# Logit products of the first layer issued four hidden units at a time, and Gelu written over its own input in a ring of nine tiles

## The chip, the core and the metric

The program runs on one NeuronCore of a Trainium2 chip. Five engines each work through their own instruction list: PE (TensorE, matrix products, with PEld for its weight loads), DVE (VectorE), ACT (ScalarE), POOL (GpSimd) and SP (SyncE, which issues DMAs). They meet only at semaphores. The metric is the device time of one execution in microseconds (us): 1949.1 us before the change, the median of three runs (1948.05 to 1950.38).

## The reference, cut to what matters

```
X  = real(fft(fft(x, axis=1), axis=2))       # x: 8 x 3072 x 256
h  = X.reshape(8*3072, 256) @ w_in           # 256 -> 2048, the first layer
g  = h * sigmoid(1.702 * h)                  # Gelu, sigmoid form
y  = g @ w_out                               # 2048 -> 256
logits = y @ w_gate                          # 8 experts
# each token goes to its best expert (capacity 768 per expert, the first tokens win),
# which computes relu(y @ w1[e]) @ w2[e], scaled by the softmax weight
```

Only tokens that an expert keeps need the second layer in full. So the program first computes just the logits of all 24,576 tokens (with `wog = w_out @ w_gate`, 2048 x 8), routes, and then recomputes the kept tokens.

## The kernel before, in words

The start (to about 93 us) loads the tables and transforms the first batch. Phase 3 (from about 1098 us) gathers the kept tokens and runs both layers for them. Between them lies phase 2, where the change is: for 8 batches of four blocks it computes the hidden values and the logits, while the transform of the next batch and the routing of the last one are threaded in between by a timetable (`pre` and `post`, numbered by unit). There is no scheduler: every engine runs its instructions in the order in which the Python code issues them.

A block holds 384 columns (385 in the fourth). One *unit* (`m1_unit`) is one of 16 slices of 128 hidden features over the block's columns. On PE it is three matmuls into a bank `pe` (L744; a fourth, L746, where a table of modes says 2) and three into a bank `po` (L749). There are two banks of each. Then `e` is formed by ACT (L752, mode 2) or DVE (L754, mode 1), and DVE writes `h = e + po` and `h = e - po` (L756, L757), 2 x 384 values. One unit later ACT issues Gelu (L763, `m1_gelu`), from a ring of three tiles `h` into a ring of six tiles `g`.

The logit products (`m1_logits`, L772) are four matmuls for a pair of units: 8 logits, padded to 32 weight columns, so each uses a strip of 32 of the array's 128 columns, and the four (two units, two signs) go to the four strips and accumulate in one bank `acc` over the block's eight pairs. The operands are float32, and the trace shows each such matmul as two instructions, so eight per pair. `flush_logits` issues one pair; the loop calls it after every odd unit, 256 times in all, for the pair whose Gelu was issued by then. After a block's last pair ACT copies `acc` out (`m1_evac`, L782).

Other names that the timetable puts between units on PE: L523 (`pf`, the transform), L707 and L709 (`psuv`, transposes of the next block's input), L722 (`psb`), L810 (`psL`) and L844 (`psp`), both routing, L425 and L431 (`pss`, a scale).

Of the kernel before, what the change touches and what calls it, by code (L numbers as in the profile page):

```python
# [10 lines left out]
F32 = mybir.dt.float32  # L11
# [11 lines left out]
P = 128  # L23
# [37 lines left out]
SEQ0 = (("uee", "vee", "row", "ueo", "veo", "w", "uo", "w"), ("vo",))  # L61
TICKS, WAIT0 = range(0, 13, 2), (2, 0, 1, 0, 1, 0, 1, 0)
AGE = (0, 2, 4, 5)


def split16(t):
# [113 lines left out]
class K:  # L180
# [128 lines left out]
    def first_folds(self):  # L309

        nc = self.nc
        ve, ge = nc.vector, nc.gpsimd
        o = FOFF
        xs = [self.xt.pop((0, i)) for i in range(6)]
        r = self.xr.pop(0)
        for i, x in enumerate(xs + [r]):
            n = P if i < 6 else 12
            jk = self.hp.tile([P, 2, 386], F32, tag="h", bufs=3, name="jk").rearrange("p s n -> p (s n)").bitcast(F16)
            v = x.rearrange("p s d -> p (s d)") if i < 6 else x
            nc.scalar.activation(jk[:n, :v.shape[1]], v, AF.Abs, accum_out=self.acc[:n, i:i + 1])  # L320
            yield
        scale = self.fft_scale(0)
        late = []
        for c in range(3):
            pe, mo, m, a = [self.xp.tile([P, 2, 2, w], F32, tag=nm, bufs=n, name=nm)
                            for nm, w, n in (("pe", UW, 1), ("mo", VW, 2), ("m", XW, 2), ("a", XW, 1))]
            eu, ev = [self.xp.tile([P, 2, w], F32, tag=nm, bufs=n, name=nm) for nm, w, n in (("eu", UW, 2), ("ev", VW, 1))]
            f = self.f[0, c] = self.fp.tile([P, FW], F32, tag="f", bufs=3, name="f")
            two = lambda k: f[:, o[k]:o[k + 1]].rearrange("p (s n) -> p s n", s=2)

            def op(e, out, x, y, sub):
                e.tensor_tensor(out, x, y, op=ALU.subtract if sub else ALU.add)
                if c == 2 and e is ve:
                    next(scale, None)

            for z in range(2):
                x = xs[2 * c + z]
                op(ge if z else ve, m[:, z], x[:, :2], x[:, 2:], True)
                op(ve, a[:, z], x[:, :2], x[:, 2:], False)
            for fn in late:  # L340
                fn()
            late = []
            op(ve, pe, a[:, :, :, :UW], a[:, :, :, UW:], False)
            if c == 2:
                op(ve, mo, m[:, :, :, 1:1 + VW], m[:, :, :, UW + 1:UW + 1 + VW], True)
            op(ve, eu, pe[:, :, 0], pe[:, :, 1], False)
            e = ge if c == 2 else ve
            op(e, two(0), pe[:, :, 0], pe[:, :, 1], True)
            e = ge if c == 1 else ve
            op(e, f[:, o[2]:o[3]], eu[:, 0], eu[:, 1], False)  # L350
            op(e, f[:, o[3]:o[4]], eu[:, 0], eu[:, 1], True)
            if c < 2:
                op(ve, mo, m[:, :, :, 1:1 + VW], m[:, :, :, UW + 1:UW + 1 + VW], True)

            def odd(c=c, f=f, mo=mo, ev=ev, two=two(1)):
                e = ve if c == 2 else ge
                op(ge, two, mo[:, :, 0], mo[:, :, 1], False)
                op(e, ev, mo[:, :, 0], mo[:, :, 1], True)
                op(e, f[:, o[4]:o[5]], ev[:, 0], ev[:, 1], True)
                op(e, f[:, o[5]:o[6]], ev[:, 0], ev[:, 1], False)  # L360

            if c == 1:
                late.append(odd)
            else:
                odd()
            del f
        for _ in scale:
            pass
        fr = self.f[0, 3] = self.fp.tile([12, UW + VW], F32, tag="fr", name="fr")
        ge.tensor_tensor(fr[:, :UW], r[:, :UW], r[:, UW:], op=ALU.add)  # L370
        ge.tensor_tensor(fr[:, UW:], r[:, 1:1 + VW], r[:, UW + 1:UW + 1 + VW], op=ALU.subtract)
        yield
        for _ in self.fft_split(0):
            pass
# [359 lines left out]
    def m1_unit(self, b, i, f):  # L734


        nc = self.nc
        n, n2 = self.blk(i)
        x = self.uvt[b, i]
        mode = (MODES0 if b == 0 else MODES7 if b == B - 1 else MODES)[NFC * i + f]  # L740
        fs = slice(f * P, (f + 1) * P)
        pe = self.peo.tile([P, 512], F32, tag="pe", bufs=EB, name="pe")
        for q, (a, c) in enumerate(((0, 0), (0, 1), (1, 0))):
            nc.tensor.matmul(pe[:, :n2], self.G[:, 0, a, fs], x[:, 0, c, :n2], start=(q == 0), stop=(q == 2 and mode != 2))  # L744
        if mode == 2:
            nc.tensor.matmul(pe[:, :n2], self.g3[:, fs], self.u3[b, i][:, :n2], start=False, stop=True)  # L746
        po = self.peo.tile([P, 512], F32, tag="po", bufs=EO - EB, name="po")
        for q, (a, c) in enumerate(((0, 0), (0, 1), (1, 0))):
            nc.tensor.matmul(po[:, :n2], self.G[:, 1, a, fs], x[:, 1, c, :n2], start=(q == 0), stop=(q == 2))  # L749
        e = self.ocp.tile([P, 386], F32, tag="e", bufs=3, name="e")  # L750
        if mode == 2:
            nc.scalar.activation(e[:, :n], pe[:, :n], AF.Copy)  # L752
        else:
            nc.vector.scalar_tensor_tensor(e[:, :n], self.ub[b, i][:, :n], self.cf[:, f:f + 1], pe[:, :n], op0=ALU.mult, op1=ALU.add)  # L754
        h = self.hp.tile([P, 2, 386], F32, tag="h", bufs=3, name="h")
        nc.vector.tensor_tensor(h[:, 0, :n], e[:, :n], po[:, :n], op=ALU.add)  # L756
        nc.vector.tensor_tensor(h[:, 1, :n], e[:, :n], po[:, :n], op=ALU.subtract)  # L757
        return h

    def m1_gelu(self, b, i, f, h):  # L760
        n, n2 = self.blk(i)
        g = self.gp.tile([P, 2, 386], F32, tag="g", bufs=6, name="g")
        self.nc.scalar.activation(g[:, :, :n], h[:, :, :n], AF.Gelu_apprx_sigmoid)  # L763
        return g

    def m1_logits(self, b, i, q, gs, acc):
        nc = self.nc
# [236 lines left out]
    def phase2(self):  # L1004
        nc = self.nc
        self.lt, self.info, self.addr = {}, {}, {}
        blocks = [(b, i) for b in range(B) for i in range(4)]

        self.parts = [[([(0, 3, 0)], 0, 3)], [([(3, 3, 0)], 3, 3)], [([(6, 3, 0)], 6, 3)],
                      [([(9, 3, 0), (0, 4, 1), (4, 4, 1), (8, 4, 1)], 9, 15)]]  # L1010
        self.whole = [([(0, 4), (4, 4), (8, 4)], 0, 24)]
        gs, pend, after = {}, [], []
        clears = self.clears()
        hprev = None
        accs = {}

        def flush_logits():
            j, q, tiles = pend.pop(0)
            b, i = blocks[j]
            if q == 0:  # L1020
                accs[j] = self.bank("acc", "acc")
            self.m1_logits(b, i, q, tiles, accs[j])
            if q == NFC // 2 - 1:
                after.append((b, i, accs.pop(j)))

        def evac():
            while after:
                b, i, acc = after.pop(0)
                self.m1_evac(b, i, acc)

        def gelu(hp):
            j, f, h = hp
            gs.setdefault((j, f // 2), []).append(self.m1_gelu(*blocks[j], f, h))
            if f % 2 == 1:
                pend.append((j, f // 2, gs.pop((j, f // 2))))

        pre, post = self.timetable()

        def take(todo):
            while todo:  # L1040
                next(todo.pop(0), None)

        for j, (b, i) in enumerate(blocks):
            for f in range(NFC):
                if j == 0:
                    next(self.conv, None)
                evac()
                take(pre[NFC * j + f])
                h = self.m1_unit(b, i, f)
                if hprev is not None:  # L1050
                    gelu(hprev)
                hprev = (j, f, h)
                del h
                if len(pend) > 1 or (pend and f % 2 == 1):
                    flush_logits()
                if j == 0:
                    next(self.conv, None)
                take(post[NFC * j + f])
                if f == 8 and j >= 4:
                    next(clears, None)  # L1060
        gelu(hprev)
        while pend:
            flush_logits()
        evac()
        self.last_route()

    def last_route(self):
# [15 lines left out]
        ps = self.bank("pf", "psO", [P, 3, 4])  # L1083
        for c in range(nt):
            if c % 4 == 0:
                q = self.gp.tile([P, 2, 386], F32, tag="g", bufs=6, name="oneh").rearrange("p s n -> p (s n)").bitcast(F16)
            oh = q[:, c % 4 * BS:c % 4 * BS + BS]
            nc.vector.tensor_scalar(oh, self.slot, self.p0[:, c:c + 1], None, op0=ALU.is_equal)
            next(pos, None)
# [309 lines left out]
```

## Time and profile before

| | us |
|---|---|
| median of three runs | 1949.1 |
| the profiled execution | 1947.09 |
| its span in the trace | 1945.3 |
| PE busy | 1882.2 (97%) |
| DVE busy | 1340.1 (69%) |
| ACT busy | 1026.9 (53%) |
| L772, busy as a group | 225.9 |
| L763 (Gelu), busy | 432.2 |

The profile is of one execution. Busy time counts overlapping instructions once. The matmuls of PE are pipelined and their ends are modelled, so what PE really spends on a piece of work is read from one start to the next. DVE and ACT rows are one instruction each unless a count says otherwise.

### The profile page before, as it was taken

What the parts mean: (1) busy time and instruction counts of PE and PEld (TensorE: products, weight loads), DVE (VectorE), ACT (ScalarE), POOL (GpSimd) and SP (SyncE); (2) the same over time, 40 slices, a digit from 0 to 9 for tenths busy, and PEclk for the clock granted to TensorE, in tenths of its full rate; (3) what the DMA queues carried; (4) which work ended last, traced back from release to release, by engine and by line L of the source; (5) the groups of instructions that cost most, each with busy time, mean ns of one, the idle gap of its engine ahead of it and who ended that gap; (6) DMA issues with size and microseconds to landing.
All of it is one profiled execution on the core that took longest, in us unless ns stands there. A gap on an engine that the chain in (4) does not pass through costs nothing.

```text
span 1945.3 us, 34942 instructions
## 1 busy us (share of the span) xinstructions
PE 1882.2 (97%) x13287; PEld 1623.3 (83%) x13287; DVE 1340.1 (69%) x2813; ACT 1026.9 (53%) x1852; POOL 654.1 (34%) x781
## 2 busy tenths in 40 slices
PE   3899999999999999999999799999999999999998
PEld 3777777777777777777777499999999999999998
DVE  9977788888988989888888755444545454544442
ACT  4577676766867767667578433332323333333322
POOL 7673538075281560832207431111100011111101
PEclk9899999999999999999999899999999999999999
DMA  8531322321333223220212011010101010111000
GB/s 264 174 114 55 106 66 82 104 76 54 107 100 107 64 61 107 81 96 15 74 41 64 26 45 50 23 55 17 55 15 44 25 49 28 37 33 43 23 9 17
DMA packets 101129, 126.71 MB, mean 65 GB/s; under 512 B 14749, under 2 KB 85941, under 8 KB 100961
## 3 DMA queue, kind: packets, MB, share of 16 engines
q1 hardware_dynamic: 88906, 111.58, 18.0%
q0 software_dynamic: 10752, 12.56, 2.4%
q8 instruction: 104, 1.70, 0.4%
q14 instruction: 63, 0.52, 0.1%
q10 hardware_dynamic: 1304, 0.35, 0.1%
HBM read 78.04 MB, written 47.64 MB: 65 GB/s over the span
## 4 chain that ended last, share of the span: by engine, by line
PE 89%; DVE 5%; issue 2%; DMA 1%; POOL 1%; ACT 1%; SPq 0%; POOLq 0%; ACTq 0%; DVEq 0%
PE pe L744 15%; PE po L749 13%; PE py L1180 13%; PE pkh L1166 13%; PE acc L772 10%; PE pod L1213 7%; PE pku L1199 7%; PE pf L523 6%; PE pe L746 2%; PE psuv L707 2%; PE psb L722 1%; PE psL L810 1%; POOL table L896 1%; DVE h L757 1%; DVE h L756 1%
## 5 line engine op out<-in xcount | busy, mean ns | idle before, releaser
L763 ACT ACTIVATE g<-h 128x768 f32<-128x768 f32 (+1 forms) x512 | 432.2, 844 | 194.1 <-DVE h L757 166.4
L744 PE MATMUL pe<-uvt,G 128*128 128x384 f32 (+1 forms) x1536 | 386.5, 360 | 1.2 <-DVE e L754 1.2
L749 PE MATMUL po<-uvt,G 128*128 128x384 f32 (+1 forms) x1536 | 352.9, 338 | 0.4 <-DVE z L869 0.2
L756 DVE TENSOR_TENSOR h<-e,po 128x384 f32<-128x384 f32 (+1 forms) x512 | 283.4, 554 | 82.9 <-ACT e L752 32.9
L1166 PE MATMUL pkh<-kx,G 128*128 128x384 f32 x1536 | 310.7, 340 | 0.1
L1180 PE MATMUL py<-kg,wo 128*128 128x384 f32 x1536 | 306.5, 336 | 0.0
L744 PEld LDWEIGHTS pe<-uvt,G 128*128 128x128 f32 x1536 | 255.0, 189 | 58.6 <-issue 31.3
L1223 POOL DMA_INDIRECT out_dram<-ko,tl x48 | 50.5, 1053 | 689.1 <-ACT ko L1222 679.3
L757 DVE TENSOR_TENSOR h<-e,po 128x384 f32<-128x384 f32 (+1 forms) x512 | 280.5, 548 | 0.0
L749 PEld LDWEIGHTS po<-uvt,G 128*128 128x128 f32 x1536 | 276.0, 189 | 2.2 <-PE pe L746 1.0
L1180 PEld LDWEIGHTS py<-kg,wo 128*128 128x128 f32 x1536 | 271.5, 188 | 0.0
L1169 ACT ACTIVATE kgf<-pkh 128x384 f32<-128x384 f32 x256 | 126.1, 493 | 268.8 <-PE pkh L1166 180.3
L1166 PEld LDWEIGHTS pkh<-kx,G 128*128 128x128 f32 x1536 | 265.0, 190 | 0.8 <-ACT kx L1156 0.5
L1170 DVE CAST kg<-kgf 128x384 fp32r<-128x384 f32 x256 | 96.4, 376 | 217.4 <-ACT kgf L1169 216.5
L896 POOL DMA_INDIRECT table<-info,ad x192 | 190.4, 992 | 127.0 <-DVE ad L890 81.0
L772 PE MATMUL acc<-g,wog 128*32 128x384 f32 (+1 forms) x2048 | 225.9, 498 | 0.4 <-ACT g L763 0.4
L754 DVE SCALAR_TENSOR_TENSOR e<-ub,cf,pe 128x384 f32<-128x384 f32 (+1 forms) x312 | 190.5, 611 | 43.9 <-PE pe L744 41.5
L1201 ACT ACTIVATE krl<-pku 128x384 fp32r<-128x384 f32 x128 | 63.0, 492 | 197.8 <-PE pku L1199 197.8
L1202 DVE SCALAR_TENSOR_TENSOR krl<-pku,krl 128x384 fp32r<-128x384 f32 x128 | 71.4, 558 | 138.6 <-ACT krl L1201 138.6
L1213 PE MATMUL pod<-w,krl 128*128 128x256 f32 x1152 | 156.5, 280 | 0.0
L1199 PE MATMUL pku<-ky,w 128*128 128x384 f32 x768 | 155.8, 338 | 0.6 <-ACT ky L1187 0.4
L1213 PEld LDWEIGHTS pod<-w,krl 128*128 128x128 f32 x1152 | 152.1, 188 | 0.0
(213 smaller groups left out, 2401.8 us busy)
## 6 DMA issues: line engine op xcount, KB each, us to landing
xc<-in_x_dram SPq DMA_DIRECT2D x48, 520.0 KB
out_dram<-zero SPq DMA_DIRECT2D x24, 1024.0 KB
stage<-in_w_dram SPq DMA_DIRECT2D x64, 256.0 KB
rt<-uvflat SPq DMA_DIRECT2D x32, 384.0 KB
f<-in_w_in_dram SPq DMA_DIRECT2D x7, 512.0 KB
f<-in_w_out_dram SPq DMA_DIRECT2D x7, 512.0 KB
uvflat<-ra SPq DMA_DIRECT2D x24, 128.0 KB
table<-info,ad POOLq DMA_INDIRECT x192, 2.1
```

The lines of the kernel that those rows point to most:

```text
L744: nc.tensor.matmul(pe[:, :n2], self.G[:, 0, a, fs], x[:, 0, c, :n2], start=(q == 0), stop=(q == 2 and mode != 2))
L749: nc.tensor.matmul(po[:, :n2], self.G[:, 1, a, fs], x[:, 1, c, :n2], start=(q == 0), stop=(q == 2))
L754: nc.vector.scalar_tensor_tensor(e[:, :n], self.ub[b, i][:, :n], self.cf[:, f:f + 1], pe[:, :n], op0=ALU.mult, op1=ALU.add)
L756: nc.vector.tensor_tensor(h[:, 0, :n], e[:, :n], po[:, :n], op=ALU.add)
L757: nc.vector.tensor_tensor(h[:, 1, :n], e[:, :n], po[:, :n], op=ALU.subtract)
L763: self.nc.scalar.activation(g[:, :, :n], h[:, :, :n], AF.Gelu_apprx_sigmoid)
L772: nc.tensor.matmul(acc[c:c + 32, :n], self.wog[:, 2 * q + j, :], gs[j][:, s, :n], start=(q == 0), stop=(q == NFC // 2 - 1))
L896: ins = nc.gpsimd.indirect_dma_start(out=self.table, out_offset=bass.IndirectOffsetOnAxis(ap=self.addr[b, t0][:, c:c + 1], axis=0), in_=se ...
L1166: nc.tensor.matmul(ps[:, :BS], self.G[:, h, a, fs], x[:, h, c], start=(q == 0), stop=(q == 5))
L1180: nc.tensor.matmul(self.py[n][k][:, :BS], self.wo[:, f, a, k * P:(k + 1) * P], g2[:, c], start=(f == 0 and a == 0 and c == 0), stop=(f == ...
L1199: nc.tensor.matmul(ps[:, :BS], w1[:, k, a, fs], y[:, k, c], start=(q == 0), stop=(q == 5))
L1213: nc.tensor.matmul(ps, r[:, c, t * P:(t + 1) * P], w2[:, F, a, :], start=(F == 0 and c == 0 and a == 0 and t != 1), stop=(F == F2 // P - 1 ...
```

## The change: what it does

`LOGITS = 4`: the loop now calls `flush_logits` only after units 1, 5, 9 and 13 of a block, and then for every pair that waits, which is two pairs (the last two pairs of a block are issued after unit 1 of the next one, and at the very end together). Gelu is written over its own input, and the tile is taken from one ring of nine, built of the three `h` buffers and the six `g` buffers in turn. The same nine tiles of memory are used. No computation is added or left out.

```diff
+HP, GP, LOGITS = 3, 6, 4
...
-        h = self.hp.tile([P, 2, 386], F32, tag="h", bufs=3, name="h")
+        h = self.hidden_tile()
         nc.vector.tensor_tensor(h[:, 0, :n], e[:, :n], po[:, :n], op=ALU.add)
         nc.vector.tensor_tensor(h[:, 1, :n], e[:, :n], po[:, :n], op=ALU.subtract)
         return h
 
+    def hidden_tile(self):
+
+        k, self.hn = self.hn % (HP + GP), self.hn + 1
+        if k < HP:
+            return self.hp.tile([P, 2, 386], F32, tag="h", bufs=HP, name="h")
+        return self.gp.tile([P, 2, 386], F32, tag="g", bufs=GP, name="g")
+
     def m1_gelu(self, b, i, f, h):
         n, n2 = self.blk(i)
-        g = self.gp.tile([P, 2, 386], F32, tag="g", bufs=6, name="g")
-        self.nc.scalar.activation(g[:, :, :n], h[:, :, :n], AF.Gelu_apprx_sigmoid)
-        return g
+        self.nc.scalar.activation(h[:, :, :n], h[:, :, :n], AF.Gelu_apprx_sigmoid)
+        return h
...
-                if len(pend) > 1 or (pend and f % 2 == 1):
-                    flush_logits()
+                if f % LOGITS == 1:
+                    while pend:
+                        flush_logits()
```

On PE, in the first units of a batch, before the change (`pe` and `po` are the two banks of a unit, `acc` the logits, `pss` a step of the scale):

```order
2096 L744 MATMUL pe<-uvt,G 128x384 x3
2097 L746 MATMUL pe<-u_4693,g_78 128x384
2098 L749 MATMUL po<-uvt,G 128x384 x3
2099 L772 MATMUL acc<-g,wog 32x384 x4
2100 L744 MATMUL pe<-uvt,G 128x384 x3
2101 L746 MATMUL pe<-u_4693,g_78 128x384
2102 L749 MATMUL po<-uvt,G 128x384 x3
2103 L431 MATMUL pss<-sc,ones 128x1
2104 L744 MATMUL pe<-uvt,G 128x384 x3
2105 L746 MATMUL pe<-u_4693,g_78 128x384
2106 L749 MATMUL po<-uvt,G 128x384 x3
2107 L772 MATMUL acc<-g,wog 32x384 x4
```

The same engine and units after the change (line numbers are 1 to 7 higher):

```order
1361 L745 MATMUL pe<-uvt,G 128x384 x3
1362 L747 MATMUL pe<-u_2787,g_78 128x384
1363 L750 MATMUL po<-uvt,G 128x384 x3
1364 L745 MATMUL pe<-uvt,G 128x384 x3
1365 L747 MATMUL pe<-u_2787,g_78 128x384
1366 L750 MATMUL po<-uvt,G 128x384 x3
1367 L432 MATMUL pss<-sc,ones 128x1
1368 L745 MATMUL pe<-uvt,G 128x384 x3
1369 L747 MATMUL pe<-u_2787,g_78 128x384
1370 L750 MATMUL po<-uvt,G 128x384 x3
1371 L779 MATMUL acc<-g,wog 32x384 x8
```

The group of four logit matmuls between the first two units has gone, and the group after the third has eight. So it is everywhere in phase 2: 256 groups of four become 128 of eight, and nothing else on PE changes its place.

On DVE, in a batch's first block, with the semaphores that each row waits for, before the change (`h` of L756 and L757 is the hidden tile; `ni`, `n` and `uvt` are routing and the next block's input):

```order
884 L882 TENSOR_SCALAR ni<-ni 128x24
885 L754 SCALAR_TENSOR_TENSOR e<-ub,cf,pe 128x384 [waits PE_49]
886 L756 TENSOR_TENSOR h<-e,po 128x384 [waits DVE_49,PE_49,Activation_49]
887 L757 TENSOR_TENSOR h<-e,po 128x384
888 L884 SCALAR_TENSOR_TENSOR n<-ni 128x24
889 L713 TENSOR_TENSOR uvt<-psuv,uvt 128x384 [waits Activation_49]
```

And after it:

```order
884 L889 TENSOR_SCALAR ni<-ni 128x24
885 L755 SCALAR_TENSOR_TENSOR e<-ub,cf,pe 128x384 [waits PE_49]
886 L757 TENSOR_TENSOR h<-e,po 128x384 [waits DVE_49,PE_49]
887 L758 TENSOR_TENSOR h<-e,po 128x384
888 L891 SCALAR_TENSOR_TENSOR n<-ni 128x24
889 L714 TENSOR_TENSOR uvt<-psuv,uvt 128x384 [waits Activation_49]
```

The order on DVE is the same. The first write of a hidden tile no longer waits for ACT (for the Gelu of three units before, which read the same buffer); it waits for PE, where its buffer was last read by the logit products of the unit nine before.

## Rows read from the trace of the kernel before

**Rows 1.** The page's first part: busy time of each engine.
```profile
PE 1882.2 (97%) x13287; PEld 1623.3 (83%) x13287; DVE 1340.1 (69%) x2813; ACT 1026.9 (53%) x1852; POOL 654.1 (34%) x781
```
**Rows 2.** Windows: start, phase 2, phase 3; length, busy us per engine (instructions), clock.
```profile
0.00:93.00 93.00, 55.80 (x472) 50.72 (x476) 85.32 (x124) 47.09 (x92) 67.17 (x72) 0.93 0.71 226
93.00:1098.00 1005.00, 998.37 (x7669) 749.05 (x7669) 855.28 (x1833) 709.11 (x1200) 468.79 (x599) 1.00 0.25 77
1098.00:1945.30 847.30, 828.07 (x5153) 823.54 (x5150) 399.46 (x857) 270.71 (x561) 118.16 (x111) 0.99 0.11 33
```
**Rows 3.** Waits of PE for a bank, 150 to 1090 us: total, times, longest.
```profile
PE pe L744 <- DVE e L754: 1.2, 1, 1.2
```
**Rows 4.** Groups by line: count, busy us, mean ns, idle before, releasers.
```profile
L772 PE MATMUL acc<-g,wog 128*32 128x384 f32 (+1 forms) x2048 | 225.9, 498 | 0.4 <-ACT g L763 0.4
L772 PEld LDWEIGHTS acc<-g,wog 128*32 128x32 f32 x2048 | 42.0, 108 | 70.5 <-issue 49.9 <-ACT g L763 16.4 <-ACT r L544 1.7
L763 ACT ACTIVATE g<-h 128x768 f32<-128x768 f32 (+1 forms) x512 | 432.2, 844 | 194.1 <-DVE h L757 166.4 <-PE po L749 8.5 <-DVE ov L887 7.9
L676 ACT ACTIVATE w<-stage 128x512 fp32r<-128x512 f32 x64 | 39.9, 624 | 0.0
L220 ACT ACTIVATE f<-f 128x512 f32<-128x512 uint32 x14 | 9.5, 681 | 3.6 <-DMA f<-in_w_in_dram 3.3 <-DMA f<-in_w_out_dram 0.3
```
**Rows 5.** Timeline of PE, 513.9 to 516.8 us: start, length to last end, instructions.
```profile
513.99 0.69 PE L749 MATMUL po<-uvt,G 128*128 128x384 f32 x3
514.61 0.85 PE L772 MATMUL acc<-g,wog 128*32 128x384 f32 x8
515.39 0.80 PE L744 MATMUL pe<-uvt,G 128*128 128x384 f32 x3
516.03 0.34 PE L746 MATMUL pe<-u,g 128*128 128x384 f32 x1
516.20 0.69 PE L749 MATMUL po<-uvt,G 128*128 128x384 f32 x3
516.73 0.69 PE L744 MATMUL pe<-uvt,G 128*128 128x384 f32 x3
```
**Rows 6.** Timeline around the group at 514.61: last four matmuls, weight loads, youngest Gelu.
```profile
514.96 0.51 PE L772 MATMUL acc<-g,wog 128*32 128x384 f32 x4
514.61 0.16 PEld L772 LDWEIGHTS acc<-g,wog 128*32 128x32 f32 x8 [0.25 <-issue]
513.42 0.84 ACT L763 ACTIVATE g<-h 128x768 f32<-128x768 f32 x1
```
**Rows 7.** Timeline of PE: transform products right behind a logit group.
```profile
534.66 0.23 PE L523 MATMUL pf<-hi,t_uo 128*128 128x129 f16 x1
534.73 0.22 PE L523 MATMUL pf<-lo,t_uo 128*128 128x129 f16 x1
534.79 0.28 PE L523 MATMUL pf<-hi,t_uo 128*128 128x129 f16 x2
```
**Rows 8.** Timeline of PE: a group that waits inside; a routing product that waits.
```profile
510.36 1.67 PE L772 MATMUL acc<-g,wog 128*32 128x384 f32 x8
504.20 0.32 PE L844 MATMUL psp<-oh,c_tri 128*128 128x192 f16 x2 [0.38 <-DVE u L730]
```
**Rows 9.** Windows, as rows 2: a usual block; half a block behind it; the last block.
```profile
600.00:630.20 30.20, 29.82 (x215) 22.43 (x211) 25.52 (x64) 21.24 (x37) 1.31 (x1) 1.00 0.45 157
630.20:644.70 14.50, 14.50 (x91) 10.32 (x89) 14.22 (x32) 13.61 (x25) 0.00 (x0) 1.00 0.00 1
1065.20:1097.00 31.80, 29.50 (x182) 20.20 (x178) 29.47 (x68) 22.22 (x40) 20.27 (x19) 1.00 0.15 39
```
**Rows 10.** Timeline of PE and DVE: a bank `po` filled, read, and filled again.
```profile
801.08 0.69 PE L749 MATMUL po<-uvt,G 128*128 128x384 f32 x3
802.86 0.55 DVE L757 TENSOR_TENSOR h<-e,po 128x384 f32<-128x384 f32 x1
804.96 0.69 PE L749 MATMUL po<-uvt,G 128*128 128x384 f32 x3
```

More of the change, by code (lines that the diff above doesn't have):

```diff
@@ L317, in first_folds @@
             n = P if i < 6 else 12
-            jk = self.hp.tile([P, 2, 386], F32, tag="h", bufs=3, name="jk").rearrange("p s n -> p (s n)").bitcast(F16)
+            jk = self.hp.tile([P, 2, 386], F32, tag="h", bufs=HP, name="jk").rearrange("p s n -> p (s n)").bitcast(F16)
             v = x.rearrange("p s d -> p (s d)") if i < 6 else x
@@ L1006, in phase2 @@
         self.lt, self.info, self.addr = {}, {}, {}
+        self.hn = 0
         blocks = [(b, i) for b in range(B) for i in range(4)]
@@ L1085, in last_route @@
             if c % 4 == 0:
-                q = self.gp.tile([P, 2, 386], F32, tag="g", bufs=6, name="oneh").rearrange("p s n -> p (s n)").bitcast(F16)
+                q = self.gp.tile([P, 2, 386], F32, tag="g", bufs=GP, name="oneh").rearrange("p s n -> p (s n)").bitcast(F16)
             oh = q[:, c % 4 * BS:c % 4 * BS + BS]
```

## The prediction

> **What bounds the kernel now.** I read the page's first part, then the span cut into its three stages, then PE's waits in the middle one, then the timeline. PE is busy for 97% of the span [rows 1]. In phase 2, where the change is, PE is busy for 998.37 of 1005.00 us at the full clock, 2.4 GHz, while DVE has 855.28 (85%) and ACT 709.11 (71%) [rows 2]. PE hardly waits: for a bank that DVE has to empty, 1.2 us in 940 [rows 3]. So over most of phase 2 what PE spends from one start to the next sets the time, and DVE and ACT follow. Phase 3 is untouched by the change, and so is the start, except that the clearing of a few shared banks shifts by a unit or two in the first block.
>
> PE's busy time is no measure of what a piece costs, since ends are modelled and overlap. The reader is to look at starts. Three matmuls of the full array in a row, then the next: 516.20 to 516.73, so 0.53 us or 0.18 each [rows 5]. That is the undisturbed pace. With a logit group behind them, the same three take from 513.99 to 514.61, 0.62 us: the group starts 0.09 late. In the group the first four matmuls start together and the last four at 514.96 [rows 6], 0.35 later: four strips side by side, two rounds of 0.35. Two rounds would end at 515.31; the next full-array matmul starts at 515.39 [rows 5], 0.08 late. And that first matmul is slow: from 515.39 to the fourth one at 516.03 it is 0.64 us instead of 0.53, 0.11 more, because its weights were not loaded ahead. So going over to strips and back costs 0.17 us beside the rounds, and 0.11 more where full-size float32 products come next.
>
> **The change part by part.**
>
> *Fewer groups.* 256 groups become 128; the last two stand back to back before as after, so 127 changeovers go. 127 x 0.17 = 21.6 us. What stands behind a removed group, counted in PE's order: 53 times L744, 34 times a transform product (L523), 31 times the transposes (L707), 7 times the routing product (L844), twice a product of the weight conversion. Behind L744 the slow start goes: 53 x 0.11 = 5.8. Behind a group the transform products start at 534.66, 534.73 and 534.79 [rows 7], only 0.01 more at the first: 34 x 0.01 = 0.3. For the transposes I have no undisturbed pair to set beside them, so they lie between these two, 0.3 to 3.4 us for 31; I take the middle, 0.06 each, 1.9. The other nine I put at nothing. Sum: 29.6 us, 0.23 per removed group. The two rounds of the second pair are not saved; they move two units later. That sum assumes that its eight instructions follow the first eight at the same 0.35 per round; no place in this trace shows sixteen in stride, hence a rival below.
>
> *What of it is not had.* First, stretches where DVE sets the pace. A usual block has DVE at 25.52 of 30.20 us, but the half block behind it has 14.22 of 14.50 and the last block 29.47 of 31.80 [rows 9]. The dense half comes in six batches, two removed groups each; with five in the last block and a half that is 17 groups, 17 x 0.23 = 4.0 us. Second, the seven removed groups in front of the routing product: it waits for DVE behind them anyway (0.38 us idle [rows 8]), so 7 x 0.17 = 1.2. Left: 29.6 - 4.0 - 1.2 = 24.4 us.
>
> *Waits of a group for Gelu.* The youngest Gelu that a group needs is of the same age as before (two units back). In a merged group the older pair goes first, which puts 0.70 us of work ahead of that wait; the group that is gone took 0.70 + 0.23 away. So the wait is met 0.23 us earlier. Shown at 514.61: that Gelu ended at 513.42 + 0.84 = 514.26 [rows 6], 0.35 us of room, which becomes 0.12. Were all 128 groups late by the 0.23, 29 us would go, the whole gain; I take nothing. On the other side, seven removed groups, one in a batch, now wait inside and last 1.67 us instead of 0.85 [rows 8]; there the wait goes, 7 x 0.82 = 5.7 us. These lie in the dense halves, so I expect DVE to keep it and count none; both ends stay in the range.
>
> *Gelu in place.* Same function, shape and count, 844 ns [rows 4]. The nearest pair of rows is a copy from one tile to another, 624 ns for 512 columns, and a scaling copy that writes over its input, 681 [rows 4]. If the 9% were due to that, ACT would be busy 39 us more, 748 of 1005; still below PE. I know no reason for a gain. I take zero.
>
> *The ring of nine.* A unit's tile is read by the logits at most five units later and written again nine units later: four units of room, 4 x 1005/512 = 7.9 us. DVE's old wait for Gelu goes, the new one for PE is met long before. Zero.
>
> *Copying `acc` out* follows a group that is 0.70 us longer, once in a block: ACT may stand 31 x 0.70 = 22 us longer, with 296 us idle in phase 2 [rows 2]. What queues behind it is one Gelu and perhaps one `e`, which DVE waits for; zero, or part of the next rival.
>
> Against the profiled execution: 1947.1 - 24.4 = 1922.7. The median shown is 2.0 above it, so the forecast is **1925 us**. With DVE keeping nothing, the transposes at their upper end and the seven waits gone: 29.6 + 1.5 + 5.7 = 36.8, so 1912.
>
> **Rivals.**
>
> *The second pair is not in stride.* Eight more weight loads have to get in while strips are running. A load is 108 ns [rows 4]; one exposed per group is 128 x 0.11 = 14 us, one per round 28 us: 1939 or 1953. Against it: all eight loads of a group took from 514.61 to 514.77 [rows 6], done 0.19 us before the second round began, so loads for the second round do get in beside running products. The strips' buffers are then full until the second round starts, and there are 0.35 us in each round for 0.11.
>
> The Trainium skill, "TensorE: Matmul & The Clock Gate", section "Part 3: Packing small matmuls — row/col tiling", says that weight loads overlap running matmuls only when the row group differs. Here all strips use all rows; by that rule one load would lie open in every round, and the time would be the 1953 of this rival. The rows just named disagree with it, so it gets a small chance.
>
> *DVE takes half.* PE runs ahead between groups (a unit after a removed group starts 0.93 us sooner), and finds its bank still full more often than in the 17 places. A bank `po` filled at 801.08 was read out by 802.86 + 0.55 = 803.41, and filled again at 804.96: 1.55 us of room [rows 10], more than 0.93. In the dense halves there is less. If half of the 24.4 went so, 1937.
>
> *The long group starves DVE, and the kernel is slower.* A group lasts 0.70 us longer, in which DVE and ACT get no new unit. Where DVE has caught up by then, it idles, and where DVE sets the pace that idle time comes back as a wait of PE three units later. It decides from 0.23 us lost per merged group. If half of the 0.70 were lost at all 128, that is 45 - 30 = 15 us slower: 1964. For it: DVE at 85%, dense in places. Against it: the room of 1.55 us, and DVE's two writes of `h` alone, 0.55 us each [rows 10], are more per unit than the added 0.70, so with one filled bank in stock it does not run dry.
>
> That the groups aren't merged can be left out: PE's order shows 128 groups of eight.
>
> **Chances.** The forecast, 1915 to 1933: 0.68. More gain (below 1915): 0.06. DVE takes half (1933 to 1942): 0.12. Not in stride: 0.08, split between its two prices. Starved: 0.06. A measurement of this kernel tells 0.2% (3.9 us) from no change; faster is 0.68 + 0.06 + 0.12 + 0.04 = 0.90, within it 0.05 (the other 0.04, and a mild starving), slower 0.05. The range that leaves out under 2 in 10 and takes in both bounds of the unknown terms: 1913 to 1941.
>
> **What would show it.** In the profile after: the L779 products should start in four rounds 0.35 us apart, with one late start and one late end per eight; phase 2 should be 20 to 30 us shorter, with PE still at 99% and DVE near 87%; the dense halves should keep their length. A fifth round's worth of time inside a group, or PE waiting for `e` or `h` by more than some 10 us in total, would prove the rivals right. A Gelu row above 0.9 us would show that in place costs. Wrong altogether would be a phase 2 as long as before.

## The result, and the profile after

The changed kernel takes **1922.8 us** (1921.6 to 1924.4), the kernel before 1948.6 us on the same chip: a ratio of 0.987, 95% interval 0.9855 to 0.9884. The forecast was 1925 us. The profiled execution's span is 1919.8 us, 25.5 shorter than before.

The page's first part and the three stages, cut at the same instructions as before (answers to [rows 1, 2]):

```profile
PE 1844.6 (96%) x13287; PEld 1636.9 (85%) x13287; DVE 1327.9 (69%) x2813; ACT 1023.4 (53%) x1852; POOL 653.9 (34%) x781
```
```profile
0.00:91.40 91.40, 53.40 (x464) 48.42 (x465) 83.54 (x121) 45.62 (x90) 65.70 (x71) 0.94 0.69 223
91.40:1071.30 979.90, 963.43 (x7675) 765.50 (x7673) 844.64 (x1836) 706.85 (x1201) 469.47 (x600) 1.00 0.25 80
1071.30:1919.80 848.50, 827.74 (x5153) 822.99 (x5150) 399.72 (x857) 270.93 (x561) 118.69 (x111) 0.99 0.11 33
```

The reader is to see that the whole difference stands in phase 2: 979.90 us for 1005.00. PE is busy for 98.3% of it instead of 99.3%, DVE for 86%. So PE's work shrank by 35 us (998.37 to 963.43) and 10 us of new gaps opened. Some of the shrinking is modelled ends, so next come the starts.

Timeline of PE: a merged group by its first half (start, length to the last end, instructions), and another by its second half. The group at 609.29 stands whole, with its weight loads (answers to [rows 5, 6]):

```profile
532.43 0.51 PE L779 MATMUL acc<-g,wog 128*32 128x384 f32 x1
532.44 0.51 PE L779 MATMUL acc<-h,wog 128*32 128x384 f32 x1
...
532.78 0.49 PE L779 MATMUL acc<-g,wog 128*32 128x384 f32 x1
...
533.86 0.79 PE L745 MATMUL pe<-uvt,G 128*128 128x384 f32 x3
```
```profile
516.64 1.16 PE L779 MATMUL acc<-h,wog 128*32 128x384 f32 x9
517.31 0.49 PE L779 MATMUL acc<-g,wog 128*32 128x384 f32 x1
...
517.63 0.49 PE L779 MATMUL acc<-h,wog 128*32 128x384 f32 x1
...
518.07 0.61 PE L723 MATMUL psb<-uvt,selr 128*128 128x384 f32 x2
```
```profile
609.29 0.16 PEld L779 LDWEIGHTS acc<-g,wog 128*32 128x32 f32 x8 [0.25 <-issue]
609.29 1.50 PE L779 MATMUL acc<-g,wog 128*32 128x384 f32 x16
609.64 0.13 PEld L779 LDWEIGHTS acc<-g,wog 128*32 128x32 f32 x4 [0.19 <-ACT g L770]
609.96 0.13 PEld L779 LDWEIGHTS acc<-g,wog 128*32 128x32 f32 x4 [0.19 <-issue]
```

Round one to round two: 532.43 to 532.78, 0.35 us. Round three to four: 517.31 to 517.63, 0.32. The loads for rounds three and four enter at 609.64 and 609.96, that is 0.35 us behind the group's start and 0.32 behind that, each with the start of the round ahead of theirs. Sixteen instructions run in stride, four rounds and no fifth. From 532.43 to the next full-array product at 533.86 are 1.43 us; two groups of before took 0.78 each from start to next start [rows 5]. So a removed group gives back 2 x 0.78 - 1.43 = 0.13, and 0.09 of late start: 0.22 us, with the 0.11 of a slow first L745 beside it where that is what followed. The three transposes (`psuv`), for which the prediction took a middle, take 0.303 us from their start to the next product behind a group, and 0.245 in the places that the change freed of one: 0.06 saved, as taken.

The costliest groups by line (answers to [rows 4]; L763 is now L770):

```profile
L770 ACT ACTIVATE g<-g 128x768 f32<-128x768 f32 (+1 forms) x341 | 288.2, 845 | 117.5 <-DVE g L758 116.2
L770 ACT ACTIVATE h<-h 128x768 f32<-128x768 f32 (+1 forms) x171 | 144.4, 844 | 61.9 <-DVE h L758 61.1
L779 PE MATMUL acc<-g,wog 128*32 128x384 f32 (+1 forms) x1364 | 155.0, 492 | 0.4 <-ACT g L770 0.4
```

Gelu in place: 845 and 844 ns, as before. Then PE's waits for a bank, 93 to 1075 us (total, times, longest; answers to [rows 3]), and the routing product of [rows 8]:

```profile
PE psp L851 <- DVE u L731: 7.7, 7, 1.2
PE po L750 <- DVE h L758: 2.3, 4, 1.6
PE po L750 <- DVE g L758: 1.9, 6, 0.8
...
PE pe L745 <- DVE e L755: 1.0, 1, 1.0
```

What has grown is `psp`: seven waits, 7.7 us. In the kernel before there were six, 2.3 us (one of them is in [rows 8]):

```profile
PE psp L844 <- DVE u L730: 2.3, 6, 0.4
```

Rows of the timeline around one of the seven:

```profile
610.72 0.62 PE L723 MATMUL psb<-uvt,selr 128*128 128x384 f32 x2
611.17 0.69 PE L745 MATMUL pe<-uvt,G 128*128 128x384 f32 x3
611.90 0.61 DVE L755 SCALAR_TENSOR_TENSOR e<-ub,cf,pe 128x384 f32<-128x384 f32 x1 [0.96 <-PE pe L745]
612.61 0.56 DVE L757 TENSOR_TENSOR h<-e,po 128x384 f32<-128x384 f32 x1
613.09 0.55 DVE L758 TENSOR_TENSOR h<-e,po 128x384 f32<-128x384 f32 x1
613.55 0.47 DVE L468 SCALAR_TENSOR_TENSOR x<-h,c_mask,fr 12x258 f16<-12x258 f16 x1
613.95 0.60 DVE L731 SCALAR_TENSOR_TENSOR u<-psb,c_pick,u3h 128x384 fp32r<-128x384 f32 x1
614.60 0.33 PE L851 MATMUL psp<-oh,c_tri 128*128 128x192 f16 x2 [1.17 <-DVE u L731]
```

Read it from the end. `psp` takes the one bank `mi`, which `psb` holds until `u` (L731) has read it. `u` stands on DVE behind the three operations of unit 14; these wait for that unit's products, and they stand on PE behind the group of sixteen (609.29 to 610.7). DVE runs dry meanwhile (0.96 us idle at 611.90). From `psb` to `psp` are 3.88 us. In the kernel before, to the `psp` of [rows 8] at 504.20, there were 3.89:

```profile
500.31 0.62 PE L722 MATMUL psb<-uvt,selr 128*128 128x384 f32 x2
```

It is a chain through two engines, and PE enters it no sooner: unit 14 starts 26.6 us into block 16 before as after (626.63 and 611.17), since the merged group ahead of it has done a pair more by then. The group that stood in front of `psp` is gone, and its time has become the wait.

The blocks show where the gain stayed. A block is measured from its first L745 to the next block's; blocks 16 to 19 stand for the middle six batches, which agree within 0.1 us, before as after:

| us | 16 | 17 | 16+17 | 18 | 19 | 30+31 |
|---|---|---|---|---|---|---|
| before | 30.12 | 31.07 | 61.19 | 32.71 | 32.02 | 63.17 |
| after | 30.14 | 29.58 | 59.72 | 31.48 | 30.91 | 64.48 |

In all, the removed groups are worth 29.6 us by the prediction's list, and 0.05 more for each of 127, so 36.0: 0.28 each, 1.1 a block. Blocks 18 and 19 got that (1.2 and 1.1). The pair 16+17 should have had 8 x 0.28 and the 0.82 us of a group that waits no more, 3.1; it got 1.5. Blocks 30 and 31 lost 1.3 where 2.0 were due.

Windows, as [rows 9]: block 16, the half block behind it, the last 33 us. Then DVE alone (length, busy, clock) from `e` of unit 14 to the first `h` of unit 23, before and after:

```profile
584.57:614.71 30.14, 28.98 (x214) 22.77 (x211) 25.89 (x66) 21.89 (x38) 1.31 (x1) 1.00 0.46 159
614.71:627.87 13.16, 13.16 (x90) 10.65 (x89) 12.89 (x29) 12.60 (x24) 0.00 (x0) 1.00 0.00 1
1038.00:1071.05 33.05, 29.19 (x188) 20.17 (x189) 29.42 (x67) 22.17 (x39) 20.17 (x19) 1.00 0.13 37
```
```profile
627.35:644.26 16.91, 16.53 (x37) 1.00 0.00 1
611.90:628.71 16.81, 16.43 (x36) 1.00 0.00 1
```

The half block is 1.3 us shorter, but DVE has three instructions less in it (29 for 32 [rows 9]): it is cut at a start of PE, which runs further ahead of DVE there, and the three come behind the cut. So such a half is no unit to count in; the pair is. DVE's own stretch shows what ends it: DVE is busy for 98% of 16.8 us, and they were 16.9 before. Two removed groups lie in these units, one of them the one that waited inside (0.82 us): 1.4 us were due, and DVE kept all but 0.1.

### The profile page after: what moved, and what is told of

The parts are those of the page before. It is cut to its first block, busy times and chain, and to the rows that moved or that the text cites. A ratio compares the mean times of both kernels' runs of the same rounds, so it can differ in the third digit from the quotient of the medians.

```text
span 1919.8 us, 34818 instructions
## 1 busy us (share of the span) xinstructions
PE 1844.6 (96%) x13287; PEld 1636.9 (85%) x13287; DVE 1327.9 (69%) x2813; ACT 1023.4 (53%) x1852; POOL 653.9 (34%) x781
## 4 chain that ended last, share of the span: by engine, by line
PE 84%; DVE 9%; issue 3%; ACT 2%; DMA 1%; POOL 0%; SPq 0%; POOLq 0%; DVEq 0%; ACTq 0%
PE pkh L1175 14%; PE py L1189 13%; PE pe L745 12%; PE po L750 12%; PE acc L779 8%; PE pod L1222 7%; PE pku L1208 7%; PE pf L524 6%; PE psuv L708 1%; PE pe L747 1%; DVE g L758 1%; PE psb L723 1%; DVE g L757 1%; DVE lo L480 1%; PE psL L817 1%
## 5 line engine op out<-in xcount | busy, mean ns | idle before, releaser
L745 PE MATMUL pe<-uvt,G 128*128 128x384 f32 (+1 forms) x1536 | 380.7, 356 | 1.0 <-DVE e L755 1.0
L770 ACT ACTIVATE g<-g 128x768 f32<-128x768 f32 (+1 forms) x341 | 288.2, 845 | 117.5 <-DVE g L758 116.2
L750 PEld LDWEIGHTS po<-uvt,G 128*128 128x128 f32 x1536 | 273.6, 188 | 11.2 <-DVE h L758 3.7
L745 PEld LDWEIGHTS pe<-uvt,G 128*128 128x128 f32 x1536 | 258.3, 189 | 25.5 <-issue 20.6
L757 DVE TENSOR_TENSOR g<-e,po 128x384 f32<-128x384 f32 (+1 forms) x341 | 188.6, 553 | 40.7 <-ACT e L753 14.7
L758 DVE TENSOR_TENSOR g<-e,po 128x384 f32<-128x384 f32 (+1 forms) x341 | 187.1, 549 | 0.0
L770 ACT ACTIVATE h<-h 128x768 f32<-128x768 f32 (+1 forms) x171 | 144.4, 844 | 61.9 <-DVE h L758 61.1
L779 PE MATMUL acc<-g,wog 128*32 128x384 f32 (+1 forms) x1364 | 155.0, 492 | 0.4 <-ACT g L770 0.4
```

The source lines that it names most:

```text
L770: self.nc.scalar.activation(h[:, :, :n], h[:, :, :n], AF.Gelu_apprx_sigmoid)
L779: nc.tensor.matmul(acc[c:c + 32, :n], self.wog[:, 2 * q + j, :], gs[j][:, s, :n], start=(q == 0), stop=(q == NFC // 2 - 1))
```

## The experiments

The first four ran on another chip, on which the kernel before takes 1.5% longer (1978.5 us). In their traces that is one place: block 26 takes 57 to 59 us for 31.5 to 32.7, there PE stands idle or has a granted clock of 1.2 GHz, and no row shows why. They are read by their ratio to before there, and by blocks.

**The ring alone.** Nine tiles and Gelu in place, groups of two units:

```
-HP, GP, LOGITS = 3, 6, 4
+HP, GP, LOGITS = 3, 6, 2
```


> Only the ring of nine and Gelu in place; the logit products are issued pair by pair after every odd unit, as before. Theory (changeovers of the strip products pay for the gain): 256 groups of four as before, so the time of before, 1948.6 us within 3, with the seven late groups of 1.67 us still there. Rival (the gain comes from the freed wait of DVE for Gelu and of Gelu for a tile): about 1923 us, as with the whole change.

Measured: 1978.8 us, ratio 0.9996 (0.9986 to 1.0005); blocks 17 and 18 at 31.06 and 32.70, as before. The ring and the writing in place are worth nothing by themselves.

**The grouping alone**, in the kernel before, with its separate tiles for `h` and `g`:

```
-                if len(pend) > 1 or (pend and f % 2 == 1):
-                    flush_logits()
+                if f % 4 == 1:
+                    while pend:
+                        flush_logits()
```


> Only the grouping of four units; three tiles h and six tiles g as before, Gelu from one into the other. Theory: the whole gain, 1923 us within 3, since the Gelu of a unit needs a tile that was read one unit earlier at the latest; ACT may wait a little at the tiles. Rival (the ring pays): 1945 to 1949 us.

Measured: 1955.1 us, ratio 0.9878 (0.9861 to 0.9894). The whole gain comes from the grouping. Blocks 16 to 18 are those of the changed kernel (30.19, 29.57, 31.52); block 19 took 31.47, not 30.91. The next experiment shows the same with the new ring (31.42), so the ring isn't the reason. In both PE waits 0.3 us there for a bank `po` that DVE empties late; why it is late stays open.

**A group ahead of the routing product**, after unit 15 again, and none between units 13 and 14:

```
-                if f % LOGITS == 1:
+                if f in ((1, 5, 11, 15) if j % 4 == 0 else (1, 5, 9, 13)):
```


> As the changed kernel, but in the first block of each batch the groups stand after units 1, 5, 11 and 15 (one, two, three and two pairs) instead of 1, 5, 9 and 13, so that a group stands again in front of the routing product that waits for DVE. The number of groups is the same. Theory (the lost part of the gain is the wait of that product, which grew from 0.38 to 1.17 us in six blocks and to 0.65 in a seventh): that wait is 0 to 0.4 us again, and the time is 4 to 6 us under the changed kernel, 1917 to 1919 us. Rival (DVE ends that block whatever PE does): the wait turns up a unit or two later, 1922 to 1924 us.

Measured: 1954.9 us, ratio 0.9874 (0.9858 to 0.9891). The `psp` waits are gone from the list, and the pair 16+17 takes 59.89: nothing gained. My theory that these waits were a loss by themselves fell. The rival comes nearer: units 3 and 4 of block 17 now take 1.58 and 1.68 us on PE for 1.23 each, so the time turns up there. (The first group of block 16 holds two pairs, not one; the first of block 17 holds one.)

**Groups of eight units**, with the nine tiles:

```
-HP, GP, LOGITS = 3, 6, 4
+HP, GP, LOGITS = 3, 6, 8
```


> As the changed kernel, but groups of four pairs, after units 1 and 9 only; the ring stays at nine tiles, so DVE must wait for the group before it can write the hidden tile of the unit just before it. Theory of changeovers: 64 fewer at 0.28 us, 18 us, but the wait for tiles and the routing product take some of it: 1908 to 1920 us. Rival (a long group starves DVE): a group of 2.7 us, and DVE idle in it by more than 0.3 us on average, so 1925 to 1950 us.

Measured: 1969.1 us, ratio 0.9949 (0.9932 to 0.9965), so most of the gain is lost again. Pair 16+17: 61.12; block 18: 32.50; only block 19 (30.93) is like that of groups of four. PE's waits for banks:

```profile
PE psp L851 <- DVE u L731: 11.8, 7, 1.8
...
PE po L750 <- DVE g L758: 6.7, 16, 0.9
...
PE po L750 <- DVE h L758: 3.6, 7, 1.6
```

That is the starving of DVE which the prediction had as its third rival; at eight units it decides. The other cause that the expectation names, DVE waiting for a tile that the group still reads, is small by the trace: 4.1 us in 11 waits. Part of the last two blocks' 67.0 us is a granted clock that fell there (0.70 over 1070 to 1075 us).

The others ran on two chips, where before takes 1948.4 and 1948.5 us.

**The steps behind a unit moved ahead of the group:**

```
+                late = j > 0 and f > 8
-                if f % LOGITS == 1:
+                if f % LOGITS == 1 and not late:
...
                 take(post[NFC * j + f])
+                if f % LOGITS == 1 and late:
+                    while pend:
+                        flush_logits()
```


> As the changed kernel, but after units 9 and 13 (from the second block on) the timetable's steps, among them the transposes psuv and the product psb for the next block, are issued on PE ahead of the group of sixteen instead of behind it. Theory (what is lost in a batch's first block is the time that ACT and DVE get no work while the group runs, and the chain from psb over ACT and DVE to the routing product, which needs psb's bank): the wait of the routing product, 1.17 us, falls under 0.2, and the first two blocks of six batches end 0.5 to 1.2 us sooner each, 3 to 7 us, less 1 to 2 us for slower starts of the unit behind the groups: ratio to the kernel before 0.983 to 0.986. Rival (DVE has no idle time to win there): the wait goes but turns up at a bank; ratio 0.987 to 0.989, and the first two blocks of a batch within 0.3 us of those of the changed kernel, 59.7 us together.

Measured: 1923.6 us, ratio 0.9873 (0.9856 to 0.9889), no different. The `psp` waits stayed at 7.7 us in seven, and block 16 became 30.61. The theory missed: `psb` now stands ahead of the group and starts 1.05 us earlier in the block, but `u` is still behind unit 14's sums on DVE, and those behind the group.

**The routing product one unit later:**

```
-ROUTE = [2, -3, 3, -4, 4, -5, 5, 6, 7, 8, 9, 15, -16] + list(range(16, 62))
+ROUTE = [2, -3, 3, -4, 4, -5, 5, 6, 7, 8, 9, 16, -17] + list(range(17, 63))
```


> As the changed kernel, but the routing product psp and the steps behind it stand one unit later. Theory (PE only waits there for the bank that psb holds): the wait falls to 0 to 0.3 us, but DVE is as late as before in the dense half behind it, so little of the 6 x 1.17 us is won, 0 to 3 us: ratio 0.985 to 0.988. Rival (the wait of PE itself is the loss): 6 to 7 us, ratio 0.983 or lower.

Measured: 1925.0 us, ratio 0.9881 (0.9865 to 0.9898). Block 16 is 1.43 us shorter and block 17 1.95 longer, pair 60.24. Waits, and the two blocks as windows:

```profile
PE pe L747 <- DVE u L731: 4.2, 7, 0.7
PE po L750 <- DVE g L758: 2.3, 6, 0.8
```
```profile
588.50:617.21 28.71, 28.71 (x212) 22.73 (x209) 24.46 (x63) 20.47 (x36) 1.31 (x1) 1.00 0.48 167
617.21:648.74 31.53, 30.31 (x232) 23.23 (x231) 29.69 (x64) 25.73 (x45) 7.65 (x8) 1.00 0.07 22
```

Now block 16 is PE's alone (28.71 of 28.71), and the wait for the same `u` comes one unit later, at L747. DVE's work is not less: 54.15 us in the pair, in 60.24.

**Groups of two units in the last two blocks:**

```
-                if f % LOGITS == 1:
+                if f % (2 if j >= 30 else LOGITS) == 1:
```


> As the changed kernel, but pair by pair again in the last two blocks, which took 64.5 us with groups of four units and 63.2 before. Theory (DVE sets the pace there, and long groups starve it): these two blocks take 62.5 to 63.5 us, 1 to 2 us less than the changed kernel; ratio within 0.001 of it. Rival (chance overlaps of a POOL operation with small DVE operations make the difference): 64 to 66 us.

Measured: 1920.5 us, ratio 0.9857 (0.9841 to 0.9873). Blocks 30+31 take 63.95 us, beside 64.52 in the next run: 0.6 us by the trace, less than I expected, and above the 62.5 to 63.5 of the theory. It is the fastest version, but its interval overlaps the next one's.

**The changed kernel again**, beside these three:

> The changed kernel itself once more, beside the three others on one chip: ratio to the kernel before 0.987 within 0.0015, and its blocks within 0.1 us of the first profile, except in the last two, where chance overlaps differ.

Measured: 1924.4 us, ratio 0.988 (0.9863 to 0.9896). Its blocks are within 0.05 us of the first profile's, except block 0 (43.98 for 45.53), which so tells nothing.

**The preparation one unit earlier**, so that `u` is ahead of unit 14's sums:

```
-PREP = (5, 9, -10, 11, -12, 13, -14, -15)
+PREP = (5, 8, -9, 10, -11, 12, -13, -14)
```


> The changed kernel with the second to the last step of each block's preparation placed one unit earlier (5, 8, 9, 10, ... for 5, 9, 10, 11, ...), so that DVE's instruction L731, which empties the bank psb, stands ahead of the sums of unit 14 and no longer behind the group of sixteen. Theory (the wait for the bank of psp is a symptom; DVE's work sets the end of the first blocks): the waits of PE at L851 fall from 7.7 us to under 2, and the first block of a batch with the one behind it stays within 0.5 us of 59.7 us; 1920 to 1925 us, ratio 0.986 to 0.989. Rival (the bank wait is the loss): the pair of blocks gets 0.8 us shorter, 1916 to 1918 us, ratio 0.984.

Measured: 1939.9 us, ratio 0.996 (0.9947 to 0.9973): 16 us slower, which neither theory had. The `psp` waits went, and the same bank is now waited for elsewhere: the scale's product `pss` (L432) waits for the copy of `uvt`. Waits; then windows of PE alone around one of them (length, busy, granted clock):

```profile
PE pss L432 <- DVE uvt L714: 11.5, 6, 2.0
PE po L750 <- DVE h L758: 3.1, 7, 1.1
```
```profile
609.00:611.00 2.00, 0.36 (x4) 1.00 1.07 384
611.00:612.00 1.00, 1.00 (x5) 0.84 1.03 419
612.00:613.00 1.00, 1.00 (x5) 0.50 1.02 413
...
616.00:617.00 1.00, 1.00 (x7) 1.00 0.88 310
```

Pair 16+17 takes 63.55 us. Behind the wait the granted clock fell from 2.4 to 1.2 GHz for some 4 us. So it did in four of the six batches; in the other two the wait is no shorter (2.0 us) and the clock stayed. The wait in the windows is the shortest of the six, 1.6 us; the others are 2.0. Block 17 is 1.4 us longer in all six, at the full clock. Windows of PE alone over blocks 4 and 8, with the product in each:

```profile
218.48:249.52 31.04, 29.07 (x214) 1.00 0.45 155
342.67:375.28 32.61, 30.64 (x213) 0.95 0.42 147
```
```profile
236.82 0.38 PE L432 MATMUL pss<-sc,ones 1*128 1x1 f32 x2 [1.97 <-DVE uvt L714]
361.04 0.38 PE L432 MATMUL pss<-sc,ones 1*128 1x1 f32 x2 [1.98 <-DVE uvt L714]
```

The same wait, one time at a clock of 1.00 over the block and one time at 0.95: 1.57 us between the two.

**The next batch's split spread over 13 units, not 11:**

```
-FSTEPS, SSTEPS, SPLIT, SSPAN, SSPAN1 = 20, 9, 13, 11, 10
+FSTEPS, SSTEPS, SPLIT, SSPAN, SSPAN1 = 20, 9, 11, 13, 10
```


> The changed kernel with the nine steps that split the next batch (ACT L478, DVE L480 and their like) spread over 13 units instead of 11, from two units earlier. Theory (DVE and ACT set the end where the split runs): the block with the split's densest part gets up to 0.7 us shorter and the one ahead of it longer by less, net 0 to 0.5 us for each of six batches, 1919 to 1924 us, ratio 0.985 to 0.988. Rival (the order of the steps around the group sets the end, not the density): no block moves by more than 0.2 us, 1922 to 1925 us.

Measured: 1927.1 us, ratio 0.9888 (0.9874 to 0.9902). Block 17 is 0.27 us shorter, block 16 1.03 longer. Both theories missed, but the size tells: one L480 (0.75 us of DVE) moved into block 16 makes it longer by 1.03. Block 16, against the window 584.57 above:

```profile
587.32:618.49 31.17, 29.79 (x214) 22.89 (x211) 26.64 (x67) 22.05 (x38) 1.31 (x1) 1.00 0.44 154
```

DVE's busy time grew by 0.75 (25.89 to 26.64) and the stretch by 1.03. DVE is busy for 85% of it, and still what is added to DVE lengthens the block: it has idle time earlier that the late work can't use. And the stretch that this L480 left, from unit 14's first `h` to unit 23's, is as much shorter: 15.35 us for 16.10 (16.19 before). That DVE's work ends this stretch is thereby shown.

**Both edits and the pairs at the end:**

> Both edits together, and groups of eight in the last two blocks. If all three are worth what their blocks say, 1916 to 1921 us, ratio 0.983 to 0.986; if DVE's work sets the end, only the last two blocks give anything: 1920 to 1923 us, ratio 0.986 to 0.987.

Measured: 1945.2 us, ratio 0.9994 (0.9984 to 1.0003), which missed both expectations; `pss` waits for 11.2 us again. The two edits add up to a kernel as slow as before, although all its groups but those of the last two blocks are merged.

## Why the prediction was right

**What bounds the kernel** (PE's starts in phase 2): right for the blocks behind the first two of a batch, which got all of the computed gain.

**Fewer groups, 29.6 us**: right in kind, 6 us too small in size. The term that was mis-sized is the round: I put 0.35 us for each, so 0.70 for the two that a merged group adds, and they add 0.65 (1.43 - 0.78). Each merged group gave 0.05 us more, so 36.0. With that, the prices of entry and exit (0.17), of the slow first product (0.11) and of the transposes (0.06) stood. That the grouping alone does it, the first two experiments showed.

**Not in stride**: did not happen. One sentence of the Trainium skill, "TensorE: Matmul & The Clock Gate", section "Part 3: Packing small matmuls — row/col tiling", lets weight loads overlap only where the row group differs, while the section's paragraph on the mechanism also names loads into a background weight buffer. Here the strips have all rows in common, and the loads of rounds three and four lie inside the rounds before them (609.64, 609.96). The measurement decides against the first of the two for these column strips.

**What DVE keeps, 4.0 and 1.2 us**: too small, and this is the step that failed. The late groups' time did go (six of 1.67 us and one, in block 1, of 1.45: 5.5 us, not 5.7), and DVE kept that and more. Gross 36.0 + 5.5 = 41.5, net 25.1, so 16.4 us were kept, where my terms and the uncounted 5.7 make 10.9. Most of the difference is one term: for the seven groups in front of `psp` I put 7 x 0.17 = 1.2 us, as if only their changeover were lost, and the waits of `psp` grew by 5.4 (2.3 to 7.7). By blocks: 1.6 in each of six pairs (9.5), 1.1 in the pair 28+29, 0.3 in block 1, 3.3 in the last two; the rest, some 2, lies in blocks 0 and 2, and block 0 differs by 1.5 between executions. I counted the groups in the dense half block and one in front of `psp`. In truth the first block of a batch kept all four of its groups' gain (30.12 to 30.14), although its DVE is busy for 85% only: its end is a chain from PE over DVE to `psp`, and from unit 14 on it belongs to the 16.8 us that DVE ends. Moving single links of the chain gave nothing (the third, fifth and sixth experiment) or cost (ninth, tenth). That the pair has a floor near 59.7 us is what these runs suggest; they don't prove it, since every one kept DVE's work as it is. Why blocks 30+31 are 0.8 us longer than before even with groups of two stays open; in the first experiment, on another chip, they took 64.0 us too.

**"The dense halves should keep their length"**: wrong as a sign to look for at PE's starts (13.16 for 14.50), for the reason told under the windows. DVE's own stretch there did keep its length (16.81 us for 16.91), so the thought behind the sign was right.

**PE waiting for `e` or `h` over some 10 us would prove the rivals right**: that did not come about. Those waits are 5.2 us, and the larger one, for `u` at `psp`, I had only as it stood (0.38 us), not as growing. DVE taking half came true in the first pairs and the last blocks alone, while the time is that of the forecast. Two errors, some 6 us of gain not seen and some 6 of loss not seen, cancelled. That is luck: the 1925 was nearer than its working deserved.

**Gelu in place, the ring**: zero, as said; shown by the first experiment.

## What to carry to other kernels

Read the price of changing between kinds of products from starts, not from busy time: 0.22 to 0.33 us here for every group that can be joined with its neighbour. Then ask for each stretch whether another engine ends it: a share of 85% over a block doesn't rule it out. Cut finer, there are 16.8 us in which that engine is busy for 98%, and that they were 16.9 before shows that nothing came of the gain there. Join until the other engine starves, and no further: here four units gave 1.3%, eight 0.5%.

## What the hardware showed beyond that

A wait of PE can cost twice: in the ninth experiment the clock was at 1.2 GHz for some 4 us behind four of six waits (one of 1.6 us, the others of 2.0), and the block 1.6 us longer. What told the four from the two these rows don't show. Behind the waits of 1.2 us in the changed kernel the clock stayed at 2.4.

Small operations of DVE in the last batch last until a tensor operation of POOL ends. Timeline of the changed kernel, the same scan twice:

```profile
1019.37 0.22 DVE L865 TENSOR_TENSOR_SCAN rs<-smask,dt 128x32 f32<-128x32 f32 x1
...
1053.64 2.81 DVE L865 TENSOR_TENSOR_SCAN rs<-smask,dt 128x32 f32<-128x32 f32 x1
1053.81 2.55 POOL L678 TENSOR_TENSOR w<-stage,w 128x512 fp32r<-128x512 f32 x2
```

0.22 us alone, 2.81 beside two POOL operations, with both ending within 0.1 us of 1056.4 (1053.64 + 2.81, 1053.81 + 2.55). In the last two blocks I count five such that last over 0.3 us longer than the shortest of their kind, and six in the profile of before, so they don't make these blocks longer than before; no experiment took them away. The Trainium skill, "SBUF — State Buffer", section "🔬 SBUF: two separate sides", describes a port pair that one of the two engines holds for a whole instruction, operations of DVE with two SBUF inputs (against a POOL operation that reads SBUF) among them, whichever starts first. That the scan ends with the POOL operations agrees with it; that it starts 0.17 us ahead of the first and yet lasts until both are done, the page doesn't explain.
